# Adaptive-LayerNorm attention with a gated MLP on one core: banks of the MLP's products, the loads of its second half, and the order of attention's last unit

## The chip, the cores and the metric

The kernel runs on one core of one Trainium2 chip. The metric is the device time in microseconds, the median of several executions; before the change it is 2931.93 us over three runs (2928.81 to 2938.05).

## The reference

A transformer block in fp32 on 2048 tokens of width 576 (`x`). A vector `c` gives six modulation rows. Attention has 32 query heads and 16 key and value heads of width 128, and looks at the last 512 cached positions; the MLP has 4608 hidden columns.

```
mod = silu(c) @ w_mod                       # sa, ca, ga, sb, cb, gb
h = layernorm(x) * (1 + ca) + sa
q = h @ wq;  p = softmax(q k^T / sqrt(128)) # k, v: last 512 positions of the caches
x = x + ga * ((p v) @ wo)
h = layernorm(x) * (1 + cb) + sb
x = x + gb * ((relu(h @ W_gate) * (h @ W_up)) @ W_down)
```

## The kernel before

**Precision.** Each fp32 operand is split into a rounded part ("hi") and a remainder ("lo"), and a product is made of three matmuls: hi by hi, hi by lo, lo by hi. ScalarE (ACT) makes the hi parts, GpSimd (POOL) the lo parts.

**Order.** The order of the instructions of TensorE (PE), VectorE (DVE), ACT and POOL is written out by hand; DMA issues on the SP queue are placed by the framework, which also hands out tiles and sets the waits. A step with a time (`step(name, t, ...)`) runs when the main loop reaches that time; unit `u` has the times `10u` to `10u + 9`. `flush` runs the work that was put off in the lists `pend` (DVE) and `pend_act` (ACT).

**Attention** is 128 units, one for each head and block of 512 queries. The loop at the end of the kernel runs for unit `u`: the scores (`s_half`), their column maxima on DVE, the next unit's query projection (`qproj`), the spread of maxima and sums by a small matmul (`spread`, tile `qm`), the maxima as a row (`max_bc`, tiles r, rh, rr, mb, mr), the exponentials (`exp_half`; in the last unit the subtraction is itself a matmul with `mr`), the hi and lo parts of p, the column sums (`ksum_op`), and P times V of unit `u - 1` (`pv_half`, twelve matmuls: for each of four key tiles two with the hi and one with the lo part). `o_mul` scales the result, `o_hi` and `o_lo` split it.

The output projection of two heads is made in "pieces" of 128 queries (`piece`, `wo_piece`, `down_piece`: twelve matmuls of 288 columns into the one pair of banks of the pool psW). A piece is either added to the accumulator `acc` by DVE, or it is "seeded": ACT first copies `acc` into the banks (`put_seed`, line 617), the matmuls add to it, and ACT copies the result back (line 593). `seeded(n)` decides which.

**The last unit** (u = 127) has no next projection; the piece of unit 123 stands in its place, and then comes the spread. Both `pv_half` of unit 126 stand behind the spread. After the last unit come the first slots of the MLP, between which unit 127's own PV, sums, scaling and split are placed (steps `T.*`), and seven pieces that were left are "fillers", taken from a list by the MLP's first block.

**The MLP.** Two halves of 1024 tokens, each of 18 blocks of 256 hidden columns: `m` is 0 to 17 in the first half, 18 to 35 in the second (NFP = 18). Each block forms its 2 x 2 products by a scheme of seven, in the order P1, P6, P2, P7, P5, P4, P3, called slots 0 to 6. A slot is 14 matmuls of 512 columns (`prod`, line 928, tile `gu`), seven for the gate and seven for the up side, with pieces of the down projection of the block before between them (`md_piece`; in blocks 19 to 34 products of its own scheme, `st_tile`). `evac` and `evac_seeded` take the finished products out of PSUM. P2 goes on in P1's banks and P3 in P5's (`heir`). In blocks 1 to 17 P4 also goes on in P7's banks, and P6 and P7 begin from a copy that ACT makes of the product before them (`seed`, line 1104).

A product's pair of banks comes from psS (two pairs, called "s") or from psX (one pair, "x", which psM held during attention); psW's pair serves the pieces. `new_pair` decides which: before, x serves P4 in block 0; P6, P7 and P4 in the second half; and in blocks 1 to 17 P5 and P6, or P1 in P6's place after a block with a LayerNorm step, with P5 on s in such blocks (LN2 = 1, 2, 4, 6) and in block 17.

**Loads.** The weights of blocks 1 to 17 are read raw, split on chip (`w_split`, lines 705 to 707), and stored; block 0 and the second half read them split, one load of 640 KB for each product (`w_prep`, line 720, tile `wop`), two slots ahead. The seven operands of a half are five tiles each (`h_back`, line 832, tiles `hop`); those of the second half take the place of the first half's. `mat(m, i, fn)` puts a step behind slot `i` of block `m`, so that it runs in the middle of the next slot. Before, the seven `h_back(1, ...)` stand at slots 0 to 6 of block 17. In block 18 the finished rows of the first half are stored on SP too (line 647), each after its last add on DVE.

Of the kernel before, what the change touches and what calls it, by code (L numbers as in the profile page):

```python
# [7 lines left out]
F32 = mybir.dt.float32  # L8
# [6 lines left out]
P = 128  # L15
# [18 lines left out]
def kernel(  # L34
# [13 lines left out]
    nc = tc.nc  # L48
# [17 lines left out]
    psM = psM_scope.__enter__()  # L66
# [341 lines left out]
    NU = HKV * NQB * 2  # L408
# [6 lines left out]
    wqs, ks, vs, wos = {}, {}, {}, {}  # L415
# [3 lines left out]
    def unit(u):  # L419
        return UNITS[u]  # L420
# [21 lines left out]
    st_, t4, t5, pt, hi_, lo_, bc, rb, rinv, ks_, pvps, done, o, bps = ({} for _ in range(14))  # L442
# [98 lines left out]
    def ksum_op(u, h):  # L541
# [4 lines left out]
        else:  # L546
            for j in range(2):
                nc.gpsimd.tensor_tensor(ks_[u], ks_[u], p[:, j, :], op=ALU.add)  # L548

    def pv_half(u, h):  # L550
        g, qb, hd = unit(u)
        if h == 0:
            pvps[u] = psM.tile([P, 512], F32, tag="mm", name=f"pv{u}")
        ps, v, a, b = pvps[u], vs[g], hi_[u, h], lo_[u, h]
        for j in range(2):
            kt = 2 * h + j
            nc.tensor.matmul(ps, v[:, kt, :], a[:, j, :], start=(kt == 0), stop=False)
            nc.tensor.matmul(ps, v[:, 4 + kt, :], a[:, j, :], start=False, stop=False)
            nc.tensor.matmul(ps, v[:, kt, :], b[:, j, :], start=False, stop=(kt == 3))
        if h:  # L560
            done[u] = pvps.pop(u)
# [37 lines left out]
    def wo_piece(u1, qt, seed=None):  # L599
        g, qb, h = unit(u1)  # L600
        return down_piece([ohi[u1 - 1], ohi[u1]], [olo[u1 - 1], olo[u1]], [wos[h - 1], wos[h]],
                          4 * qb + qt, qt, f"wo{u1}_{qt}", seed=seed)
# [4 lines left out]
    w_use, pieces, seeds = set(), [], {}  # L607

    def seeded(n):
        return 0 < n < len(pieces) and (n - 1 in seeds or pieces[n - 1][0] % 10 == 6) and not any(pieces[n - 1][0] < t <= pieces[n][0] for t in w_use)  # L610

    def put_seed(n):
        if seeded(n):
            u1, qt = pieces[n][1:]
            g, qb, h = unit(u1)
            s = seeds[n] = psW.tile([P, 2, 512], F32, tag="w", name=f"wo{u1}_{qt}")
            nc.scalar.copy(s[:, :, :H2], acc[4 * qb + qt].rearrange("p (h n) -> p h n", h=2))

    def piece(n):
        add = wo_piece(*pieces[n][1:], seed=seeds.get(n))  # L620

        def end():
            add()
            put_seed(n + 1)

        (pend_act if n in seeds else pend).append(end)
        return n in seeds
# [7 lines left out]
    NFP = NFT // 2  # L635
# [5 lines left out]
    def md_piece(m, k, qt, pool=None):  # L641
# [4 lines left out]
        if fp == NFP - 1:  # L646
# [3 lines left out]
    OPS = {"P1": ("A11", "B11"), "P2": ("A12", "B21"), "P6": ("S2", "T2"), "P7": ("S3", "T3"),  # L650
           "P5": ("S1", "T1"), "P4": ("A22", "T4"), "P3": ("S4", "B22")}

    def order(m):
        return ("P1", "P6", "P2", "P7", "P5", "P4", "P3")
# [174 lines left out]
    def h_back(b, s):  # L829
        hs = hop[b, s] = [hp.tile([P, 512], F32R, tag="hT", name=f"hop{b}_{s}_{k}") for k in range(5)]  # L830
        for k in range(5):
            nc.sync.dma_start(hs[k][:96 if k == 2 else P].bitcast(F32), hkeep[b, s, k].bitcast(F32))
# [98 lines left out]
    LN2 = (1, 2, 4, 6)  # L931
# [154 lines left out]
    def new_banks(nm, k):  # L1086
        npair[0] += 1
        return (px["x"] if k == "x" else psS).tile([P, 2, 512], F32, tag=k, name=nm)

    def new_pair(m, s):  # L1090
        x = {"P4"} if not m else {"P6", "P7", "P4"} if m >= NFP else {"P1" if m - 1 in LN2 else "P6", "P5"}
        if m in LN2 or m == NFP - 1:
            x.discard("P5")
        pair[m, s] = new_banks(f"gu{npair[0]}", "x" if s in x else "s")

    def heir(m):
        return {"P2": "P1", "P3": "P5", **({"P4": "P7"} if 0 < m < NFP else {})}
# [227 lines left out]
    for i in range(1, len(VIS)):  # L1325
        g, qbs = VIS[i]
# [40 lines left out]
    for i, ab in enumerate(lay0 + lay):  # L1367
        n = i - len(lay0) - 2 * NFT + 4
# [4 lines left out]
    def mat(m, s, fn, sums=False):  # L1373
        mextra.setdefault((m, s, sums) if s < 6 else (m + 1, -1, sums), []).append(fn)
# [17 lines left out]
        mat(*at_, fn)  # L1392
    for i, fn in enumerate(sum(later.values(), [])):
        mat(7 + i // 5, (0, 1, 2, 4, 6)[i % 5], fn)
    for i, s in enumerate(order(1)):
        mat(NFP - 1, i, lambda s=s: h_back(1, OPS[s][1]))

    def sums(m, i):

# [12 lines left out]
    def mlp_slots():  # L1412
        for m in range(NB):
            two = m - 1 in ST
            if two:
                md = st_list(m - 1)
            else:
                md = [lambda k=k, qt=qt: md_piece(m - 1, k, qt) for k in range(2) for qt in range(4)] if m else []
            for i, s in enumerate(order(m)):
                early = 0 < m < NFP and not i  # L1420
                if not early:
                    flush_stores()
                if s in heir(m):
                    pair[m, s] = pair[m, heir(m)[s]]
                elif s not in seeds_of(m):
                    new_pair(m, s)
                prod(m, s, 7 * m + i, 0)
                if (m or i) and not early:
                    sums(m, i)
                    others(m, i)  # L1430
                if m in ST and i == 0:
                    sw_load(m)
                if two or m and i:
                    md.pop(0)()
                elif filler and not m:
                    filler.pop(0)()
                for fn in mextra.pop((m, i - 1, True), []):
                    fn()
                if two and i == 0:
                    if m - 1 in ST:  # L1440
                        sw_cut(m - 1, "T2")
                if two and i < 3:
                    st_sums(m - 1, (("S1", "S3"), ("S2",), ("S4",))[i])
                if m in ST:
                    sw_prep(m, i)
                prod(m, s, 7 * m + i, 1)
                wop.pop(7 * m + i)
                if early:
                    evac_seeded(m, s)
                    if put:  # L1450
                        put.pop()()
                    flush_stores()
                    sums(m, i)
                    others(m, i)
                if two or m and i < 2:
                    md.pop(0)()
                elif filler and not i:
                    filler.pop(0)()
                if not early:
                    (evac_seeded if 0 < m < NFP else evac)(m, s)  # L1460
                yield
        for k in range(2):
            for qt in range(4):
                if qt % 2 == 0:
                    st_end(k, qt // 2)
                md_piece(NB - 1, k, qt, (psS, "s") if qt % 2 else None)
        flush_stores()
        assert not mextra and not filler

    filler = [lambda q=q: wo_piece(NU - 3, q)() for q in (1, 2, 3)]  # L1470
    mlp = mlp_slots()

    def last_unit():
# [23 lines left out]
    t = 546  # L1497
    for s in ("P1", "P2", "P4", "P7", "P5", "P6", "P3"):
        for xx in range(2):
            for fn in w_later(s, xx, (xp, "xm", 640)):  # L1500
                step("w.l", t, fn)
                t = after(t + 8)
# [40 lines left out]
    def run(u, k):  # L1543
        t = 10 * u + k
        while sched and sched[-1][0] <= t:
            fn, args = sched.pop()[2:]
            fn(*args)
# [11 lines left out]
    for u in range(NU):  # L1559
        run(u, 0)  # L1560
        if u > 1 and u % 2 == 0:
            o_hi(u - 2)
            o_lo(u - 2)
        s_half(u, 0)
        s_half(u, 1)
        max_pre(u)
        if u:
            sum_pre(u - 1)
        run(u, 1)
        if u + 1 < NU:  # L1570
            qproj(u + 1, 0, 14)
        else:
            piece(at[10 * u + 1])
        run(u, 2)
        spread(u)
        max_bc(u)
        if u + 1 < NU:
            q_hi(u + 1)
        run(u, 3)
        if 10 * u + 3 in at:  # L1580
            piece(at[10 * u + 3])
        if u > 1 and u % 2:
            o_hi(u - 2)
            o_lo(u - 2)
        run(u, 4)
        if u:
            pv_half(u - 1, 0)
        if u + 1 == NU:
            pv_half(u - 1, 1)
        flush(pend_act)  # L1590
        exp_half(u, 0)
        flush()
        run(u, 5)
        exp_half(u, 1)
        if u:
            sum_bc(u - 1)
        if u + 1 < NU:
            q_lo(u + 1)
        ksum_op(u, 0)
        ksum_op(u, 1)  # L1600
        run(u, 6)
        if 0 < u < NU - 1:
            pv_half(u - 1, 1)
        if 10 * u + 6 in at:
            piece(at[10 * u + 6])
        run(u, 7)
        if u:
            o_mul(u - 1)
        flush()
        run(u, 8)  # L1610
        hi_half(u, 1)
        flush(pend_act)
        lo_half(u, 0)
        lo_half(u, 1)
        run(u, 9)
# [56 lines left out]
```

## Time and profile before

| | |
|---|---|
| median of three runs | 2931.93 us (2928.81 to 2938.05) |
| the profiled execution | 2930.85 us |
| its span, first to last instruction | 2929.1 us |
| TensorE busy | 2858.8 us, 98% of the span |
| VectorE, ScalarE, GpSimd busy | 73%, 51%, 72% |
| mean granted TensorE clock | 0.995 |
| DMA | 396.43 MB, 135 GB/s in the mean |

Idle time of TensorE counts first; a wait names the engine and line that ended it. A name such as `gu<-hop_T,wop` is the written tile and the read ones, with buffer numbers left out. L928 is line 928 of the kernel before. A matmul's recorded end is modelled and lies after the start of the next one.

### The profile page before, as it was taken

How to read it: one execution, taken by the hardware profiler on the slowest of the kernel's cores; microseconds unless marked ns; L12 is line 12 of the kernel's file. 1: busy time of each engine (PE TensorE's matmuls, PEld its weight loads, DVE VectorE, ACT ScalarE, POOL GpSimd, SP SyncE). 2: the span in 40 equal slices, each digit the busy share in tenths (PEclk: the TensorE clock that was granted, in tenths of full speed). 3: DMA queues.
4: the chain of work that ended last, by engine and by line, in shares of the span. 5: the costliest groups of instructions: out<-in, count | busy, mean ns of one | idle time of the engine just before them, and what ended most of it. 6: DMA issues, size and time to landing. Idle time of an engine off the chain costs nothing. (4 is left out here: it accounts for less than half of the span.)

```text
span 2929.1 us, 41284 instructions
## 1 busy us (share of the span) xinstructions
PE 2858.8 (98%) x15214; PEld 2488.3 (85%) x15214; DVE 2149.0 (73%) x2980; ACT 1489.0 (51%) x2097; POOL 2108.6 (72%) x1564
## 2 busy tenths in 40 slices
PE   6799999999999999999999999999999999999999
PEld 5688888888888888888888788888888888888888
DVE  7878888788878888777889655566676466666666
ACT  4466666666666666666756344443444122222221
POOL 5588888888888889876778666677777356656553
PEclk9899999999999999999999999999999999999999
DMA  4011222222223223322244456666667944444442
GB/s 150 22 45 55 83 93 84 67 99 93 92 83 106 90 63 133 101 70 85 65 146 133 135 209 219 225 231 223 234 227 245 327 160 152 151 152 152 158 151 104
DMA packets 162697, 396.43 MB, mean 135 GB/s; under 512 B 14912, under 2 KB 61760, under 8 KB 162496
## 3 DMA queue, kind: packets, MB, share of 16 engines
q1 hardware_dynamic: 131472, 282.15, 30.3%
q10 hardware_dynamic: 31024, 111.65, 9.7%
q8 instruction: 120, 1.97, 0.3%
q14 instruction: 81, 0.66, 0.1%
HBM read 268.73 MB, written 153.32 MB: 144 GB/s over the span
## 5 line engine op out<-in xcount | busy, mean ns | idle before, releaser
L539 POOL TENSOR_TENSOR lo<-p,hi 128x1024 fp32r<-128x1024 f32 x256 | 609.7, 2403 | 0.8 <-ACT hi L519 0.8
L548 POOL TENSOR_TENSOR ks<-ks,p 128x512 f32<-128x512 f32 x256 | 343.8, 1343 | 272.9 <-ACT p L532 207.6
L460 DVE TRANSPOSE_TENSOR_REDUCE t<-s 128x32 f32<-128x1024 f32 x256 | 316.4, 1243 | 135.2 <-PE s L457 123.9
L928 PE MATMUL gu<-hop_B,wop 128*128 128x512 f32 (+1 forms) x1512 | 378.4, 393 | 0.3 <-DMA wop<-wk_P 0.3
L928 PE MATMUL gu<-hop_T,wop 128*128 128x512 f32 (+1 forms) x1260 | 321.6, 395 | 2.2 <-DMA wop<-wk_P 2.2
L383 PE MATMUL qps<-hTa,wA 128*128 128x512 f32 x1288 | 312.5, 394 | 8.7 <-ACT lfa L365 7.4
L928 PEld LDWEIGHTS gu<-hop_B,wop 128*128 128x128 f32 (+1 forms) x1512 | 275.7, 188 | 52.7 <-ACT lflh L913 0.9
L584 PE MATMUL wo<-woga,ohi 128*128 128x288 f32 x1472 | 306.0, 301 | 1.5 <-DVE lfa L363 1.5
L383 PEld LDWEIGHTS qps<-hTa,wA 128*128 128x128 f32 x1288 | 244.7, 190 | 61.3 <-ACT lfa L365 7.8
L530 DVE TENSOR_TENSOR p<-s,mb 128x1024 f32<-128x1024 f32 x246 | 290.3, 1219 | 4.1
L519 ACT CAST hi<-p 128x1024 fp32r<-128x1024 f32 x256 | 268.9, 1050 | 7.1
L595 DVE TENSOR_TENSOR acc<-md,acc 128x576 f32<-128x576 f32 x160 | 120.9, 756 | 198.9 <-PE md L584 198.6
L928 PEld LDWEIGHTS gu<-hop_T,wop 128*128 128x128 f32 (+1 forms) x1260 | 228.9, 188 | 43.8 <-issue 2.4
L584 PE MATMUL md<-wogb,hhi 128*128 128x288 f32 x1280 | 261.5, 297 | 3.3 <-DVE acc L595 2.3
L532 ACT ACTIVATE p<-p 128x1024 f32<-128x1024 f32 x246 | 259.9, 1057 | 8.0 <-DVE p L530 7.9
L435 ACT ACTIVATE qhi<-qps 128x512 fp32r<-128x512 f32 x128 | 76.4, 597 | 340.6 <-PE qps L383 340.6
L584 PEld LDWEIGHTS wo<-woga,ohi 128*128 128x128 f32 x1472 | 238.7, 188 | 9.1 <-issue 1.9
L584 PEld LDWEIGHTS md<-wogb,hhi 128*128 128x128 f32 x1280 | 214.0, 189 | 16.0 <-DVE acc L595 3.1
L1039 DVE TENSOR_TENSOR acc<-st_P,acc 128x576 f32<-128x576 f32 x160 | 121.2, 757 | 134.7 <-PE st_P L1030 133.8
L584 PE MATMUL wo<-woga,olo 128*128 128x288 f32 x736 | 216.9, 295 | 0.3 <-POOL olo L573 0.2
L584 PE MATMUL md<-wogb,hlo 128*128 128x288 f32 x640 | 189.0, 295 | 0.0
L573 POOL TENSOR_TENSOR olo<-rb,ohi 128x512 fp32r<-128x512 f32 x128 | 166.6, 1301 | 23.7 <-ACT ohi L569 23.2
(263 smaller groups left out, 7084.9 us busy)
## 6 DMA issues: line engine op xcount, KB each, us to landing
wop<-wk_P SPq DMA_DIRECT2D x133, 640.0 KB
wk_P<-wop ACTq DMA_DIRECT2D x119, 640.0 KB
wr<-wlay SPq DMA_DIRECT2D x68, 384.0 KB
rogb<-wd SPq DMA_DIRECT2D x68, 288.0 KB
againq<-akq SPq DMA_DIRECT2D x18, 640.0 KB
rwA<-wq SPq DMA_DIRECT2D x32, 320.0 KB
wlay<-wg SPq DMA_DIRECT2D x36, 256.0 KB
roga<-wo SPq DMA_DIRECT2D x32, 288.0 KB
```

The lines of the kernel that those rows point to most:

```text
L383: return [lambda i=i, a=a, b=b: nc.tensor.matmul(ps, a, b, start=(i == 0), stop=(i == n - 1)) for i, (a, b) in enumerate(ops)]
L460: nc.vector.tensor_reduce(t4[u][:, 2 * h:2 * h + 2, :].rearrange("p k b -> p (k b)"), t.rearrange("p k (b j) -> p (k b) j", j=32), axis=AX ...
L519: nc.scalar.copy(hi_[u, h], pt[u, h])
L530: nc.vector.tensor_tensor(p, t, bc[u][:, None, :].to_broadcast([P, 2, 512]), op=ALU.subtract)
L532: nc.scalar.activation(p, p, AF.Exp, bias=0.0, scale=1.0)
L539: nc.gpsimd.tensor_sub(lo_[u, h], pt[u, h], hi_[u, h].bitcast(F32))
L548: nc.gpsimd.tensor_tensor(ks_[u], ks_[u], p[:, j, :], op=ALU.add)
L573: nc.gpsimd.tensor_sub(olo[u], o.pop(u), ohi[u].bitcast(F32))
L584: nc.tensor.matmul(ps[:, half, :H2], a[:, sl], w[b][:, cs], start=(n == 0 and seed is None), stop=(n == 5), skip_group_check=seed is not None)
L595: nc.vector.tensor_tensor(av, ps[:, :, :H2], av, op=ALU.add)
L928: nc.tensor.matmul(ps, a, c, start=s not in heir(m) and i == 0 and s not in seeds_of(m), stop=i == len(ops) - 1, skip_group_check=True)
L1039: nc.vector.tensor_tensor(t, ps[:, :, :H2], t, op=ALU.add)
```

## The change

Five edits. The second half's operands of P5, P4 and P3 are loaded later, behind slot 6 of block 17 and slots 0 and 1 of block 18; those of P1, P6, P2 and P7 stand behind slots 0, 1, 3 and 4 of block 17. `new_pair` gives x to P1 (and with it P2) in every block after block 0, and to P4 as well in block 0 and in the second half; all else is on s. In the last attention unit the eight hi matmuls of unit 126's PV are issued ahead of the spread and the four lo matmuls behind it; the last piece is no longer seeded; and block 0 takes no filler in slot 3 but two in slot 4.

```diff
+    def pv_part(u, lows):
+        g, qb, hd = unit(u)
+        if not lows:
+            pvps[u] = psM.tile([P, 512], F32, tag="mm", name=f"pv{u}")
+        ps, v = pvps[u], vs[g]
+        for kt in range(4):
+            a, b = (x[u, kt // 2][:, kt % 2, :] for x in (hi_, lo_))
+            if lows:
+                nc.tensor.matmul(ps, v[:, kt, :], b, start=False, stop=kt == 3)
+            else:
+                nc.tensor.matmul(ps, v[:, kt, :], a, start=kt == 0, stop=False)
+                nc.tensor.matmul(ps, v[:, 4 + kt, :], a, start=False, stop=False)
+        if lows:
+            done[u] = pvps.pop(u)
...
     def seeded(n):
-        return 0 < n < len(pieces) and (n - 1 in seeds or pieces[n - 1][0] % 10 == 6) and not any(pieces[n - 1][0] < t <= pieces[n][0] for t in w_use)
+        return 0 < n < len(pieces) - 1 and (n - 1 in seeds or pieces[n - 1][0] % 10 == 6) and not any(pieces[n - 1][0] < t <= pieces[n][0] for t in w_use)
...
     def new_pair(m, s):
-        x = {"P4"} if not m else {"P6", "P7", "P4"} if m >= NFP else {"P1" if m - 1 in LN2 else "P6", "P5"}
-        if m in LN2 or m == NFP - 1:
-            x.discard("P5")
+        x = ("P4",) if not m else ("P1", "P4") if m >= NFP else ("P1",)
...
-    for i, s in enumerate(order(1)):
-        mat(NFP - 1, i, lambda s=s: h_back(1, OPS[s][1]))
+    for (m, i), s in zip([(NFP - 1, i) for i in (0, 1, 3, 4, 6)] + [(NFP, 0), (NFP, 1)], order(1)):
+        mat(m, i, lambda s=s: h_back(1, OPS[s][1]))
...
-                elif filler and not m:
+                elif filler and not m and i != 3:
                     filler.pop(0)()
...
-                elif filler and not i:
+                elif filler and i in (0, 4):
                     filler.pop(0)()
...
             piece(at[10 * u + 1])
+            pv_part(u - 1, False)
         run(u, 2)
         spread(u)
...
         run(u, 4)
-        if u:
+        if u + 1 == NU:
+            pv_part(u - 1, True)
+        elif u:
             pv_half(u - 1, 0)
-        if u + 1 == NU:
-            pv_half(u - 1, 1)
```

## The prediction

> **What bounds the kernel now.** I read the page first, then the table of windows by stage (columns: stretch, length, busy time of PE, PEld, DVE, ACT and POOL with instructions, clock, DMA share, GB/s), then TensorE's waits inside the stages.
>
> ```profile
> PE 2858.8 (98%) x15214; PEld 2488.3 (85%) x15214; DVE 2149.0 (73%) x2980; ACT 1489.0 (51%) x2097; POOL 2108.6 (72%) x1564
> ...
> 200.00:1600.00 1400.00, 1395.94 (x7399) 1214.16 (x7399) 1153.55 (x1703) 940.88 (x1261) 1156.70 (x718) 1.00 0.28 90
> 1600.00:1675.00 75.00, 69.03 (x364) 58.40 (x363) 52.60 (x75) 32.56 (x46) 47.66 (x31) 1.00 0.41 130
> 1675.00:2270.00 595.00, 587.30 (x3231) 516.87 (x3230) 369.90 (x370) 257.69 (x360) 433.96 (x386) 1.00 0.64 227
> 2270.00:2345.00 75.00, 72.52 (x389) 63.62 (x388) 30.35 (x38) 13.35 (x19) 22.22 (x18) 0.98 0.89 321
> 2345.00:2900.00 555.00, 555.00 (x2965) 484.76 (x2965) 360.39 (x499) 136.73 (x258) 323.27 (x319) 1.00 0.47 151
> ```
>
> TensorE sets the end. Nothing can be won from 2345 on, where it never idles. The idle time that the edits can reach is the last attention unit with block 0 of the MLP (1600 to 1675: 5.97 us), blocks 1 to 17 (7.70 us) and the change of halves, blocks 17 and 18 (2.48 us). Who ended it, stage by stage (total us, times, longest; two waits of 0.5 us in the first stage follow below in their own rows):
>
> ```profile
> PE wo L584 <- ACT ohi L569: 1.6, 1, 1.6
> PE qm L483 <- DVE t L475: 1.3, 1, 1.3
> PE wo L584 <- ACT acc L593: 1.1, 1, 1.1
> PE wo L584 <- POOL olo L573: 0.8, 1, 0.8
> ...
> PE gu L928 <- ACT gu L1104: 5.2, 7, 1.4
> PE md L584 <- DVE acc L595: 2.3, 1, 2.3
> ...
> PE gu L928 <- DMA wop<-wk_P: 2.5, 2, 2.2
> ```
>
> **What one stall costs.** A recorded wait is too small, since a matmul's end lies after its successor's usual start. Block 9 hands over without a wait, block 14 with one:
>
> ```profile
> 1971.65 0.30 PE L584 MATMUL md<-wogb,hlo 128*128 128x288 f32 x1
> 1971.78 0.40 PE L928 MATMUL gu<-hy_T,wop 128*128 128x512 f32 x1
> ...
> 2151.16 0.29 PE L584 MATMUL md<-wogb,hlo 128*128 128x288 f32 x1
> 2152.13 0.50 PE L928 MATMUL gu<-hy_T,wop 128*128 128x512 f32 x1 [0.68 <-ACT gu L1104]
> ```
>
> Start to start is 0.13 and 0.97 us, a loss of 0.84 for a recorded 0.68, and the first matmul takes 0.50 instead of 0.40. So each stall costs its record plus 0.26 us.
>
> **Part 1, the last unit and block 0.** The last unit's chain, then the fillers:
>
> ```profile
> 1624.31 4.71 POOL L539 TENSOR_TENSOR lo<-p,hi 128x1024 fp32r<-128x1024 f32 x2
> 1626.72 0.45 PE L483 MATMUL qm<-t,quad 128*128 128x80 f32 x2 [1.34 <-DVE t L475]
> 1627.21 0.22 DVE L498 TENSOR_REDUCE r<-qm 128x16 f32<-128x64 f32 x1 [0.54 <-PE qm L483]
> 1627.51 1.54 DVE L505 CAST rh<-r 128x16 fp32r<-128x16 f32 x1
> 1630.79 1.19 PE L526 MATMUL s<-mr,minus 128*128 128x512 f32 x4 [0.50 <-ACT mr L511]
> 1631.16 0.63 ACT L593 COPY acc<-wo 128x576 f32<-128x576 f32 x1
> 1631.83 0.64 ACT L617 COPY wo<-acc 128x576 f32<-128x576 f32 x1
> 1632.52 0.54 PE L584 MATMUL wo<-againo,ohi 128*128 128x288 f32 x2 [0.54 <-ACT wo L617]
> ...
> 1637.10 0.40 PE L584 MATMUL wo<-againo,ohi 128*128 128x288 f32 x1 [1.11 <-ACT acc L593]
> ...
> 2368.27 1.62 PE gu L928 x7
> ...
> L595 DVE TENSOR_TENSOR acc<-md,acc 128x576 f32<-128x576 f32 x160 | 120.9, 756 | 198.9 <-PE md L584 198.6
> ```
>
> Moving the eight high matmuls of unit 126's PV ahead of the spread: seven such matmuls issue in 1.62 us, so eight take 1.85 us from 1625.4 (1626.72 less the wait of 1.34), and the spread (qm) starts at 1627.2, not 1626.7. The wait of 1.34 is filled, but the chain to the subtraction (qm, r, rh, mr, s) begins 0.5 us later, and only four PV matmuls are left to cover it. What saves it is rh: 1.54 us for 16 columns, ending at 1629.05, just behind the POOL pair that ends at 1629.02. I read it as held by POOL; then a later r is free and s still starts at 1630.79. Value 0, bounds 0 and 0.5 us lost.
>
> The Trainium skill (SBUF — State Buffer, "SBUF: two separate sides") calls the pair of ports that VectorE and GpSimd share an exclusive lock, taken for a whole instruction by whichever comes first. By that rule the sum has 0 here, without it 0.5 us lost; the trace agrees with it in the two ends, 1629.05 and 1629.02.
>
> The last piece unseeded: ACT's copy (L617, 0.64 us) goes, and the piece can start when L593 ends, at 1631.8 to 1631.9 instead of 1632.52: 0.6 us. Its sum goes from ACT, where the copy out stood behind both exponentials, to a DVE add (L595) behind o_mul. So the first filler of block 0 no longer waits: 1.11 + 0.26 = 1.4 us.
>
> Slot 3's filler waits for unit 127's ohi and olo (1.63 + 0.81 recorded, 2.44). It moves behind two halves of a product, 2 x 1.62 = 3.24 us of other matmuls, which covers 2.44: 2.44 + 2 x 0.26 = 3.0 us. What is late next: two fillers in slot 4 are now one half (1.62 us) apart on psW's single pair, and the second waits for the first's DVE add, 0.76 us with its start some 0.3 us behind the matmul; it fits by 0.5 us. Block 0's P5 evacuation on DVE then stands behind that second add; P3, which accumulates on P5's bank, needs it a slot later. Part 1: 0.6 + 1.4 + 3.0 = 5.0 us; bounds 3 and 5.
>
> **Part 2, banks in blocks 1 to 17.** P6's start is a seed: ACT copies P1's bank into P6's. Two seeds, block 14 (P6 on the x pair) and block 5 (P6 already on psS, because block 4 ran the LayerNorm):
>
> ```profile
> 2148.30 0.84 ACT L705 CAST wop<-ws 128x768 fp32r<-128x768 f32 x1 [4.06 <-DVE ws L735]
> 2151.08 1.00 ACT L1104 COPY gu<-gu 128x1024 f32<-128x1024 f32 x1 [1.94 <-DVE u L1077]
> ...
> 1824.59 1.00 ACT L1104 COPY gu<-gu 128x1024 f32<-128x1024 f32 x1 [0.70 <-PE gu L928]
> 1825.77 0.62 ACT L1067 CAST hhi<-u 128x512 fp32r<-128x512 f32 x1 [0.19 <-DVE u L1077]
> ```
>
> In block 14 the seed waits for DVE's u, the evacuation of the previous block's P3, which held the x pair. In block 5 it starts off PE while u is still to come (1825.77): P6 took the bank that P4 left a slot earlier. The change gives every block that order: P1 on x (free since P2, slot 2), P6, P7, P5 in turn on psS. P7 then inherits P3's bank, a whole slot later. So all seven recorded waits should go: 5.2 + 7 x 0.26 = 7.0 us. Two things can hold some back. ACT runs L705, which waits for DVE's ws, ahead of the seed, and in block 14 it ended at 2149.14; unheld, P6 would start at 2151.29, so a seed of 1.00 us must start by 2150.3, a slack of 1.1 us; and DVE, gaining nothing, stays as late as it is. Bounds 2 and 7; I take 6.3, nearer to the block 5 row. The 2.3 us wait of md for DVE's acc is not touched: 0, bounds 2.6 either way, since it hangs on how VectorE and POOL happen to meet.
>
> **Part 3, the change of halves.** The stall is P6's operand wop, late behind operand loads on SP:
>
> ```profile
> 2286.71 2.37 SPq L832 DMA_DIRECT2D hop_T<-hk_T  x2
> 2290.98 0.32 SPq L720 DMA_DIRECT2D wop<-wk_P  x1
> 2292.20 3.99 SPq L832 DMA_DIRECT2D hop_T<-hk_T  x5
> ...
> 2290.00:2298.00 8.00, 5.80 (x30) 4.56 (x28) 2.84 (x4) 1.64 (x2) 1.29 (x1) 1.00 1.04 385
> 2298.00:2302.00 4.00, 3.71 (x12) 3.15 (x13) 0.00 (x0) 0.00 (x0) 0.00 (x0) 0.60 1.03 362
> ```
>
> One operand is four loads of 256 KB and one of 192 KB (the code's shapes), 1.25 MB, or 3.2 us at the 385 GB/s of that row. The new order takes T1 out from ahead of this wop, so it lands about 3.2 us sooner; it was 2.2 us late. Both waits go: 2.5 + 2 x 0.26 = 3.0 us. After the stall TensorE ran at a mean clock of 0.60 for 4 us: another (1 - 0.60) x 4 = 1.6 us. Together 4.6 us.
>
> The Trainium skill (TensorE: Matmul & The Clock Gate, "What's actually happening") has the clock halve after an idle window of about 3.4 us. By it a 2.2 us wait would have cost itself alone and this part be 3.0 us; the trace disagrees (0.60 behind a 2.2 us wait), and I keep 4.6.
>
> What is late next: in block 18 three operands, 3 x 1.25 MB, stand among four wop loads (0.66 MB each), the out stores, which wait on SP for DVE's adds, and a wogb load. At 385 GB/s the operands add about 3.2 us of queue to each slot of some 4.8 us. A wop is issued about two slots ahead, so I expect it to fit narrowly. Value 4.2; bounds 1 and 4.6.
>
> **The second half's banks.** P1 moves to x, which P4 leaves. P4's last reader in one block, and the next block's P1:
>
> ```profile
> 2567.60 0.69 DVE L1077 SCALAR_TENSOR_TENSOR srb<-srb,gu 128x512 f32<-128x512 f32 x1
> 2570.07 0.63 PE L928 MATMUL gu<-hop_B,wop 128*128 128x512 f32 x2
> ```
>
> The reader ends at 2568.29, 1.8 us ahead of P1: no cost. P6, P7 and P5 on psS have longer.
>
> **Sum.** 5.0 + 6.3 + 4.2 = 15.5 us from the profiled execution's 2930.85 us (span 2929.1 and 1.75 around it): 2915.4. That execution lies 1.1 us under the median, 2931.93, so I write 2916.
>
> **Rivals.**
> 1. VectorE and POOL set the pace of blocks 1 to 17, and part 2 yields its lower bound 2 while the rest comes: 2930.85 - 5.0 - 2 - 4.2, about 2920. For it: ws in 4.06 us of ACT idling above. Against: block 9 has no wait, and POOL is busy 434 of 595 us.
> 2. The operand loads of block 18 make a later wop late (P5 or P4), with a fresh clock drop: part 3 falls to 0, 2930.85 - 11.3, about 2920. With rival 1 too, 2924: no difference that could be told. About 0.3% (8.8 us) is what this measurement tells from none.
> 3. The change does not do what it says: the allocator hands P6 the bank of P3, not P4's. Part 2 is 0: about 2922. The block 5 rows speak against it.
> 4. Slower: in the second half P4's evacuation lands after the next P1. It decides from 1.8 us of delay. If DVE's evacuation slips by 3.3 us, two adds of 0.75 us beyond that, all 17 blocks pay 1.5 + 0.26: 30 us, twice what is won, 2915.4 + 30, about 2945. Against: TensorE has no wait there in 555 us, and DVE is busy only 360.
>
> **Numbers.** Forecast 0.62; rival 1 alone 0.12, rival 2 alone 0.09, both 0.06, rival 3 0.04, rival 4 or another new wait 0.07. Faster by over 0.3% (below 2923.1): 0.62 + 0.12 + 0.09 less a little of each edge, 0.80; within 0.3%: 0.13; slower: 0.07. The forecast's best case, 5.0 + 7.0 + 4.6 + 2.6 = 19.2, gives 2911.6, and the runs of before reach 3 us under their median: low 2909. High 2928, with rivals 1 and 2 both and one md wait more.
>
> **What would show it.** L483's wait gone and s still near 5.4 us behind the piece before it; no waits for L617, L593, ohi or olo in block 0; L1104 released by PE in every block; no wop wait and a clock of 1.00 at the change of halves; 0 idle in the second half. It is wrong if L1104 still waits for u, if wop waits return in block 18, or if gu waits for DVE in the second half.

## The result and the profile after

The changed kernel takes 2920.61 us in the median (2916.08 to 2925.96), the kernel before 2932.45 beside it: ratio 0.9958, 95% interval 0.9942 to 0.9974. It is faster, by 11.8 us where the forecast had 16, and inside the range. A later measurement of the same kernel gave 2920.13 (2916.42 to 2921.20), ratio 0.9963 (0.9949 to 0.9977).

The execution profiled first took 2925.96 us, with a span of 2923.5. In the changed kernel every line behind the new function stands 15 further down, those behind the rewritten choice of banks 13 (the product L928 is L943, md and wo L584 are L599, the DVE add L595 is L610, the DVE sums L735 are L750, POOL's wop L706 and L707 are L721 and L722, the seed L1104 is L1117, DVE's u L1077 is L1092). Below, a "seed wait" is a wait of TensorE for that copy by ACT, an "md wait" one for the banks of a down-projection piece (tile md), and a "wop wait" one for a product's weights (tile wop). The table of windows by stage, columns as before:

```profile
1600.00:1675.00 75.00, 72.89 (x381) 62.79 (x380) 55.90 (x79) 34.41 (x48) 52.02 (x32) 0.98 0.47 151
1675.00:2270.00 595.00, 590.00 (x3235) 519.90 (x3234) 384.50 (x369) 259.80 (x362) 440.54 (x387) 0.99 0.63 226
2270.00:2345.00 75.00, 74.10 (x409) 65.30 (x408) 31.25 (x41) 13.22 (x20) 23.30 (x20) 1.00 0.90 327
2345.00:2900.00 555.00, 555.00 (x2969) 485.04 (x2968) 361.14 (x501) 136.16 (x256) 323.15 (x320) 1.00 0.46 150
```

TensorE's idle time falls from 5.97 to 2.11 us in the first stage, from 7.70 to 5.00 in the second, and from 2.48 to 0.90 in the third, which makes 8.1 us; in the fourth it is still 0. But the clock, 1.00 in the first two stages before, is now 0.98 and 0.99. TensorE's waits in the first three stages:

```profile
PE pv L558 <- POOL lo L539: 1.1, 1, 1.1
PE s L526 <- ACT mr L511: 1.0, 1, 1.0
...
PE md L599 <- DVE acc L610: 4.7, 2, 2.3
PE gu L943 <- DMA wop<-wk_P: 0.9, 1, 0.9
PE gu L943 <- POOL wop L722: 0.2, 1, 0.2
```

The seven waits for ACT's seed (5.2 us before) are gone, and so are block 0's three and the one of 2.2 us for wop. The md wait for DVE's add, one of 2.3 us before, now stands there twice. In the last unit, waits of 1.1 and 1.0 us stand where 1.3 and 0.5 stood. The seed of block 14, which waited for DVE's u in the prediction's rows, now starts off TensorE while u is still to come:

```profile
2150.00 1.00 ACT L1117 COPY gu<-gu 128x1024 f32<-128x1024 f32 x1 [0.59 <-PE gu L943]
2151.30 0.62 ACT L1082 CAST hhi<-u 128x512 fp32r<-128x512 f32 x1 [0.30 <-DVE u L1092]
```

So it is in every block: P6's seed waited for u in 8 of 17 blocks before, and is released by TensorE in all 17 now.

Where the gain lies is read from starts, since busy times hide the clock. Five points of TensorE's timeline in the kernel before: the first score matmul of unit 127, the first product of block 0, the end of block 0's last product, slot 6 of block 17, and the end of block 18's last product.

```profile
1620.88 0.39 PE L455 MATMUL s<-qhi,againk 128*128 128x512 f32 x1
...
1634.22 0.85 PE L928 MATMUL gu<-hop_B,wop 128*128 128x512 f32 x3
...
1675.02 1.10 PE L928 MATMUL gu<-hop_B,wop 96*128 96x512 f32 x4
...
2285.79 0.86 PE L928 MATMUL gu<-hop_B,wop 128*128 128x512 f32 x3
...
2330.17 1.09 PE L928 MATMUL gu<-hop_B,wop 96*128 96x512 f32 x4
```

The same points in a second profiled execution of the changed kernel (2919.17 us, span 2917.4; the run e8 below):

```profile
1621.44 0.39 PE L455 MATMUL s<-qhi,againk 128*128 128x512 f32 x1
...
1634.30 0.85 PE L943 MATMUL gu<-hop_B,wop 128*128 128x512 f32 x3
...
1670.71 1.10 PE L943 MATMUL gu<-hop_B,wop 96*128 96x512 f32 x4
...
2279.07 0.86 PE L943 MATMUL gu<-hop_B,wop 128*128 128x512 f32 x3
...
2318.93 1.10 PE L943 MATMUL gu<-hop_B,wop 96*128 96x512 f32 x4
```

Their differences, with those of the first profile (the same five points there are 1623.90, 1637.74, 1674.14, 2284.01 and 2325.06):

| stretch, us | before | after, first profile | after, second profile | second less before | forecast |
|---|---|---|---|---|---|
| up to unit 127 | 1620.88 | 1623.90 | 1621.44 | +0.56 | 0 |
| last unit | 13.34 | 13.84 | 12.86 | -0.48 | -0.6 |
| block 0 | 40.80 | 36.40 | 36.41 | -4.39 | -4.4 |
| blocks 1 to 17 | 610.77 | 609.87 | 608.36 | -2.41 | -6.3 |
| change of halves | 44.38 | 41.05 | 39.86 | -4.52 | -4.2 |
| rest | 598.93 | 598.44 | 598.47 | -0.46 | 0 |
| span | 2929.1 | 2923.5 | 2917.4 | -11.7 | -15.5 |

One stretch falls well short, blocks 1 to 17. Three other things differ between two executions of one program: the start-up, which the change doesn't touch (3.0 us later in the first, 0.6 in the second), the last unit, and the change of halves.

**Why blocks 1 to 17 fall short.** Block 8 in the second profile, VectorE's timeline:

```profile
1949.26 1.23 DVE L1139 TENSOR_TENSOR c<-gu,u 128x1024 f32<-128x1024 f32 x1 [0.92 <-PE gu L943]
1950.52 0.69 DVE L1140 SCALAR_TENSOR_TENSOR c<-c 128x512 f32<-128x512 f32 x1
1951.12 6.06 DVE L750 TENSOR_TENSOR wr<-wr,wr 128x768 f32<-128x768 f32 x1
1957.11 0.74 DVE L610 TENSOR_TENSOR acc<-md,acc 128x576 f32<-128x576 f32 x1
```

POOL's in the same time:

```profile
1950.55 1.26 POOL L721 TENSOR_TENSOR wop<-wr,wop 32x256 fp32r<-32x256 f32 x1 [1.82 <-ACT wop L720]
1951.77 1.28 POOL L722 TENSOR_TENSOR wop<-wr,wop 128x512 fp32r<-128x512 f32 x1
1953.02 1.42 POOL L182 TENSOR_TENSOR wogb<-rogb,wogb 128x576 fp32r<-128x576 f32 x1
1954.41 1.28 POOL L1083 TENSOR_TENSOR hlo<-c,hhi 128x512 fp32r<-128x512 f32 x1
1955.65 0.71 POOL L721 TENSOR_TENSOR wop<-wr,wop 32x256 fp32r<-32x256 f32 x1
1956.34 1.97 POOL L722 TENSOR_TENSOR wop<-wr,wop 128x512 fp32r<-128x512 f32 x1
```

And TensorE's:

```profile
1957.91 0.54 PE L599 MATMUL md<-wogb,hhi 128*128 128x288 f32 x2 [2.33 <-DVE acc L610]
```

The sum of the weights' third quarter (wr on wr, 128x768) takes 0.94 to 0.95 us in 15 of its 17 places in this profile and 6.05 or 6.06 in two, in blocks 8 and 10; in the kernel before it is 6.06 in block 10 alone. Here it starts 0.57 us into a row of POOL instructions without a gap. Going by its own 0.95 us, an estimate, it gets through only at the last change between them, at about 1956.23; the POOL sum that starts there takes 1.97 us where the same form takes 1.28. The add of the last md piece stands behind it on VectorE, the one pair of md banks stays taken, and the next md piece waits 2.33 us. Slot 6 of block 8 is 2.61 us longer than before: the record plus 0.28. In block 10 the same wait was there before, and the slot is still 1.53 us longer. That is the clock:

```profile
1957.16:1960.57 3.41, 2.66 (x17) 2.49 (x18) 2.91 (x5) 1.46 (x2) 2.54 (x3) 1.00 0.59 238
...
2032.26:2035.67 3.41, 3.41 (x12) 2.87 (x11) 0.97 (x2) 0.84 (x2) 3.19 (x3) 0.50 0.90 312
```

Behind block 8's wait (first row) it is 1.00, behind block 10's 0.50 for 3.41 us. So 2.61 + 1.53 = 4.1 us were given back, and what is left for the removed seeds is 2.4 + 4.1 = 6.5, a remainder. In the first profile, with a half clock behind both waits, 4.00 + 1.52 = 5.5 us were given back.

### The profile page after: what moved, and what is told of

It is laid out like the page before. It is cut to its first block, busy times and chain, and to the rows that moved or that the text cites. A ratio compares the mean times of both kernels' runs of the same rounds, so it can differ in the third digit from the quotient of the medians.

```text
span 2923.5 us, 41266 instructions
## 1 busy us (share of the span) xinstructions
PE 2858.1 (98%) x15214; PEld 2490.0 (85%) x15214; DVE 2161.4 (74%) x2981; ACT 1489.4 (51%) x2095; POOL 2117.4 (72%) x1564
## 3 DMA queue, kind: packets, MB, share of 16 engines
q8 instruction: 120, 1.97, 0.3%
## 5 line engine op out<-in xcount | busy, mean ns | idle before, releaser
L943 PE MATMUL gu<-hop_B,wop 128*128 128x512 f32 (+1 forms) x1512 | 379.0, 394 | 0.9 <-DMA wop<-wk_P 0.9
L943 PEld LDWEIGHTS gu<-hop_B,wop 128*128 128x128 f32 (+1 forms) x1512 | 276.3, 188 | 53.6 <-issue 1.3
L943 PE MATMUL gu<-hop_T,wop 128*128 128x512 f32 (+1 forms) x1260 | 319.9, 393 | 0.0
L599 PE MATMUL wo<-woga,ohi 128*128 128x288 f32 x1472 | 305.9, 301 | 1.5 <-DVE lfa L363 1.5
L599 PE MATMUL md<-wogb,hhi 128*128 128x288 f32 x1280 | 263.4, 298 | 5.8 <-DVE acc L610 4.9
L943 PEld LDWEIGHTS gu<-hop_T,wop 128*128 128x128 f32 (+1 forms) x1260 | 228.4, 188 | 41.0
L610 DVE TENSOR_TENSOR acc<-md,acc 128x576 f32<-128x576 f32 x160 | 120.9, 756 | 177.5 <-PE md L599 177.1
L599 PEld LDWEIGHTS wo<-woga,ohi 128*128 128x128 f32 x1472 | 238.7, 188 | 9.1 <-issue 1.9
L599 PEld LDWEIGHTS md<-wogb,hhi 128*128 128x128 f32 x1280 | 214.9, 190 | 19.1 <-DVE acc L610 6.3
L599 PE MATMUL wo<-woga,olo 128*128 128x288 f32 x736 | 216.9, 295 | 0.3 <-POOL olo L588 0.2
L599 PE MATMUL md<-wogb,hlo 128*128 128x288 f32 x640 | 190.1, 297 | 0.0
```

The lines of the kernel that those rows point to most:

```text
L599: nc.tensor.matmul(ps[:, half, :H2], a[:, sl], w[b][:, cs], start=(n == 0 and seed is None), stop=(n == 5), skip_group_check=seed is not None)
L943: nc.tensor.matmul(ps, a, c, start=s not in heir(m) and i == 0 and s not in seeds_of(m), stop=i == len(ops) - 1, skip_group_check=True)
```

## The experiments

**Each part alone.** The banks, on the kernel before:

```diff
-        x = {"P4"} if not m else {"P6", "P7", "P4"} if m >= NFP else {"P1" if m - 1 in LN2 else "P6", "P5"}
-        if m in LN2 or m == NFP - 1:
-            x.discard("P5")
+        x = ("P4",) if not m else ("P1", "P4") if m >= NFP else ("P1",)
```

> The kernel before with the banks alone (P1 and P2 on x). Theory: the banks take away the seven seed waits (7.2 us by the slots' lengths), and nothing of the banks themselves makes TensorE wait elsewhere; the md waits of 2.3 us in slot 6 come from DVE's sum S3 being held by POOL for 6.06 us, in whatever block the two happen to meet. Then no seed wait is left, and the time falls by 7.2 us less 1.5 to 4 us for each block in which a 6.06 us sum is found (none to two): 2925 to 2931. Rival: the banks give TensorE its gain back by themselves, since the blocks' period is set by VectorE and POOL: then the freed time comes back as waits for POOL's or ACT's wop in most blocks, not in slot 6 of one or two, and the time stays within 2 us of before.

Measured 2925.84 us, ratio 0.9981 (0.9972 to 0.9991). Its waits from 1675 to 2345:

```profile
PE md L584 <- DVE acc L595: 2.6, 2, 2.3
PE gu L928 <- DMA wop<-wk_P: 2.6, 1, 2.6
```

No seed wait is left, and blocks 1 to 17 are 6.2 us shorter than in the kernel before, against part 2's 6.3. The md wait of 2.3 us is in block 10, as before; block 8 has one of 0.32.

The operand loads, on the kernel before:

```diff
-    for i, s in enumerate(order(1)):
-        mat(NFP - 1, i, lambda s=s: h_back(1, OPS[s][1]))
+    for (m, i), s in zip([(NFP - 1, i) for i in (0, 1, 3, 4, 6)] + [(NFP, 0), (NFP, 1)], order(1)):
+        mat(m, i, lambda s=s: h_back(1, OPS[s][1]))
```

> The kernel before with the later operand loads alone. Theory: P6's weight load no longer waits behind two operands, so its 2.2 us wait and the half clock behind it go; the wait of P1's load, 0.28 us before, stays, since that load still stands behind the third and fourth operand. Blocks 17 and 18 get 3.5 to 4 us shorter, and the time falls by as much (about 2928.5). Rival: the loads moved into block 18 make a later weight load wait there, and the time falls by under 1 us.

Measured 2930.35, ratio 0.9987 (0.9979 to 0.9996). The waits in the same stretch:

```profile
PE gu L928 <- ACT gu L1104: 6.2, 7, 1.5
PE md L584 <- DVE acc L595: 2.3, 1, 2.3
```

The wop waits are gone, P1's of 0.28 too, which was expected to stay. From the start of block 17 to the end of 18 it takes 3.7 us less, and 4.5 less in the table's stretch from slot 6 of block 17. The md wait is still one of 2.3, but in block 8, not 10, and with a half clock behind it: this edit touches neither the banks nor anything before block 17's loads, and the wait has moved all the same. So it is not the banks alone that place it.

The last unit, on the kernel before (the PV in two parts, the last piece unseeded; block 0's fillers as they were):

```diff
+            pv_part(u - 1, False)
...
-        if u:
+        if u + 1 == NU:
+            pv_part(u - 1, True)
+        elif u:
             pv_half(u - 1, 0)
-        if u + 1 == NU:
-            pv_half(u - 1, 1)
...
-        return 0 < n < len(pieces) and (n - 1 in seeds or pieces[n - 1][0] % 10 == 6) and not any(pieces[n - 1][0] < t <= pieces[n][0] for t in w_use)
+        return 0 < n < len(pieces) - 1 and (n - 1 in seeds or pieces[n - 1][0] % 10 == 6) and not any(pieces[n - 1][0] < t <= pieces[n][0] for t in w_use)
```

> The kernel before with the last attention unit's edits alone (PV in two parts, last piece unseeded). Theory: the two parts gather the unit's idle time into one stretch of 2 us right behind the spread, the clock halves there for 3.4 us, and block 0 starts 0.5 us later against the start of the unit than before; slot 0 is then 1.4 us shorter because the last piece is unseeded. Net 0.9 us. Rival: the half clock in the changed kernel's profile was a chance of that one execution: block 0 starts 0.6 us earlier, net 2.0 us.

Measured 2931.68, ratio 0.9995 (0.9985 to 1.0005). The last unit takes 12.84 us and slot 0 of block 0 is 1.36 shorter, together 1.9; the run as a whole can't be told from no change. The waits of 1.1 and 1.0 us (pv for POOL's lo, s for ACT's mr) are there as in the first profile of the changed kernel, but no half clock behind them. So the new place of the PV does not by itself make the half clock; the last section shows what goes with it. This profile has no md wait at all, and no sum of 6.06 us in any block, on the old banks. The edit of block 0's fillers was not run alone; its worth is read from the slots of block 0.

The changed kernel with the PV back in its old place, run twice:

```diff
-            pv_part(u - 1, False)
...
-        if u + 1 == NU:
-            pv_part(u - 1, True)
-        elif u:
+        if u:
             pv_half(u - 1, 0)
+        if u + 1 == NU:
+            pv_half(u - 1, 1)
```

> The changed kernel with the last unit's PV back behind the spread in one piece (unseeded last piece, fillers, banks and loads kept). Theory: the waits are 1.3 and 0.5 us apart again, no half clock in the last unit, and block 0 starts 1.1 to 1.3 us earlier against the unit's start than in the changed kernel. Rival: the unseeded piece makes the half clock, not the PV in two parts: it stays, and block 0 starts no earlier.

> The changed kernel with the PV of the last unit in its old place, once more. Its first profile had the 2.34 us md wait in block 10 alone (0.38 in block 8), while both profiles of the changed kernel have it in 8 and 10. If the place of that wait belongs to the program, block 8's sum takes 0.95 us here again and the median is 2917 to 2919, some 2 us under the changed kernel; if it belongs to the execution, block 8 may show 6.06 us, and the medians are the same.

Measured 2918.28, ratio 0.9948 (0.9935 to 0.9962), and 2917.25, ratio 0.9949 (0.9935 to 0.9962). The last unit takes 12.82 and 12.81 us, against 12.86 in the second profile of the changed kernel: the place of the PV is worth nothing there. Both profiles have the held sum in block 10 alone. Block 8 in the second of them, VectorE and then POOL:

```profile
1951.08 0.95 DVE L750 TENSOR_TENSOR wr<-wr,wr 128x768 f32<-128x768 f32 x1
```

```profile
1951.57 1.05 POOL L721 TENSOR_TENSOR wop<-wr,wop 32x256 fp32r<-32x256 f32 x1 [1.82 <-ACT wop L720]
1952.59 1.29 POOL L722 TENSOR_TENSOR wop<-wr,wop 128x512 fp32r<-128x512 f32 x1
```

The sum starts within 0.04 us of where it starts in the changed kernel, but POOL's row begins at 1951.57 instead of 1950.55, after the start of the sum and not before it. That one microsecond decides between 0.95 and 6.06.

The changed kernel again:

> The changed kernel itself once more, profiled again: what of its profile is the kernel's and what the execution's. The seed waits should be absent again. If the half clock behind the 2.34 us md wait and in the last unit depends on the execution, one of the three windows (last unit, block 8, block 10) is missing or has moved here; if it depends on the kernel, all three return at the same places. The same for the 3.0 us by which the last unit started later than in the kernel before. Median 2918 to 2922.

Measured 2920.13, ratio 0.9963 (0.9949 to 0.9977). The held sums return in blocks 8 and 10, as they return in block 10 alone in the pair of runs above: in two programs the place was the same twice. But the kernel with the later loads, which is the kernel before up to block 17, has its held sum in block 8 and not in 10, and of the kernel before there is one profile; what places the sum stays open. The half clock is there behind block 10 only, and not in the last unit; the start-up is 0.56 us later than before and not 3.0; P1's wop wait of 0.9 is absent. These belong to the execution.

**Moving the held sum.** The sum is issued one slot earlier, behind the md piece, on the changed kernel and on the one before:

```diff
-        for k, s in {1: [(0, "S1")], 2: [(0, "S4")], 5: [(1, "S3")], 6: [(1, "S2")]}.get(i, []):
+        for k, s in {1: [(0, "S1")], 2: [(0, "S4")], 6: [(1, "S2")]}.get(i, []):
...
+                if i == 4 and m + 1 < NFP:
+                    w_sums(m + 1, "S3")
```

> The changed kernel with one edit: the sum of the third quarter of the weights (DVE, line 750, 128x768 on wr), which runs beside the evacuation of P4's product and held DVE for 6.06 us in one block of the changed kernel's profile (0.95 us is its median), is issued one slot earlier, behind the slot's md piece. Theory A: the 2.34 us waits of md for DVE's add in blocks 8 and 10 come from this sum, which POOL holds off; then no sum on wr lasts 6 us, both waits go (5.5 us by the slots: 4.00 and 1.52), any clock drop behind them goes too, and blocks 1 to 17 come to about 604 us against 609.6: median about 2915. Rival B: POOL holds whichever two-input operation of DVE stands there; then another sum (ws) or the c of line 1140 lasts several us instead, a seed or a wop is late, and the median stays at 2919 to 2922. Rival C: the sum ahead of the evacuation of P5 makes that late, and P3, which accumulates on its bank, waits: 0.5 us a block or more, 2925 or above.

> The kernel before with the same single edit of the sum. By theory A only block 10's md wait (2.34 + 0.26 us) goes: about 2.6 us under the kernel before, ratio 0.9991, with the seven seed waits still there. By rival B no difference or a new wait of like size; by rival C slower by 5 us or more. If both this and the edit of the changed kernel gain, the md wait is a cost of its own that the change of banks neither makes nor removes.

Measured 2920.73, ratio 0.9967 (0.9954 to 0.9980), and 2940.30, ratio 1.0033 (1.0020 to 1.0047). On the changed kernel the 2.3 us waits go, but the time does not. The waits from 1675 to 2300:

```profile
PE gu L943 <- POOL wop L722: 1.0, 5, 0.4
PE md L599 <- DVE acc L610: 1.0, 3, 0.6
```

The groups of VectorE there (busy, mean ns of one):

```profile
L750 DVE TENSOR_TENSOR ws<-wr,wr 128x768 f32<-128x768 f32 x16 | 55.8, 3486 | 0.0
L1140 DVE SCALAR_TENSOR_TENSOR c<-c 128x512 f32<-128x512 f32 x17 | 38.8, 2281 | 0.6
L750 DVE TENSOR_TENSOR wr<-wr,wr 128x768 f32<-128x768 f32 x16 | 28.3, 1772 | 0.0
```

The means were 3023 (ws), 1788 (c) and 1585 ns (wr) in the second profile of the changed kernel. The c and the ws now take longer, and the moved sum itself is not free: it takes 1.7 to 4.0 us in ten of its 17 places instead of 6.06 in two. From block 1's first product to slot 6 of 17 it is 606.7 us, against 608.1; this profiled execution loses 1.2 us in the last unit, by a half clock there. Rival B is the right one: other operations are held, and small waits stand in several blocks. On the kernel before, the same edit takes the md wait of 2.3 us away too and costs 8.8 us. Its waits from 1675 to 2345:

```profile
PE gu L928 <- ACT gu L1104: 14.1, 10, 3.3
PE gu L928 <- DMA wop<-wk_P: 1.6, 1, 1.6
PE md L584 <- DVE acc L595: 0.5, 2, 0.3
```

The seed waits grow from 5.2 us in seven to 14.1 in ten, and the moved sum is held in 13 of 17 places (1.3 to 4.3 us). What ends the wait in block 6, ACT's timeline and then TensorE's (1.43 us in the kernel before):

```profile
1867.67 1.00 ACT L1104 COPY gu<-gu 128x1024 f32<-128x1024 f32 x1 [3.96 <-DVE u L1077]
```

```profile
1868.72 0.50 PE L928 MATMUL gu<-hy_T,wop 128*128 128x512 f32 x1 [3.31 <-ACT gu L1104]
```

With the old banks a later VectorE (u, L1077) is a later seed, and TensorE waits. With the new ones no seed waits for u, here or in any of the nine profiles with these banks. The same edit costs 8.8 us on the one (2940.30 less 2931.46) and 0.6 on the other (2920.73 less 2920.13), all measured side by side; those figures include the md waits of 2.3 us that the edit takes away, one on the kernel before and two on the changed one.

The sum on POOL, on the changed kernel, on it with the old place of the PV, and on the kernel before:

```diff
-        nc.vector.tensor_tensor(flat(out), flat(a), flat(b), op=op)
+        (nc.gpsimd if s == "S3" else nc.vector).tensor_tensor(flat(out), flat(a), flat(b), op=op)
```

> The changed kernel with one edit: the third-quarter sum (line 750, 128x768 on wr) runs on POOL instead of DVE, in the same place of the program. In the runs so far it takes DVE 0.95 us, or 6.06 us where it starts inside a back-to-back run of POOL; on POOL, whose 128x512 sums take 1.28 us, I estimate 1.9 us. Theory A: the md waits of blocks 8 and 10 come from VectorE standing still behind POOL in this one sum; with it off VectorE, both go (2.61 and 1.53 us of slot time in the second profile of the changed kernel), nothing else of VectorE is held as long there, and POOL, 434 busy of 595 us, has room for 17 x 1.9 us: median 2914 to 2917. Rival B: the wait only moves, since POOL's own wop (line 722) is now 1.9 us later behind the sum, or another sum of VectorE is held: wop waits on POOL of 0.3 us or more in most blocks, median 2919 to 2925.

> The same with the PV of the last unit in its old place behind the spread. By theory A and a value of 0 to 0.5 us for that place: 2913 to 2917, the fastest of all; by rival B as the run before it, 2919 to 2925.

> The kernel before with the sum on POOL. By theory A block 10's md wait goes (2.6 us), and the seed waits, which hang on VectorE's u, stay or shrink: 2925 to 2929. By rival B the seed waits grow, as they did with the sum one slot earlier (14.1 us against 5.2): 2932 to 2942. What the change of banks is worth is then the distance to the changed kernel with the same edit: about 8 to 12 us if the seeds stay, more if they grow.

Measured 2930.55, ratio 0.9995 (0.9986 to 1.0004); 2931.05, ratio 0.9995 (0.9986 to 1.0004); and 2949.20, ratio 1.0060 (1.0047 to 1.0073). All of the gain is lost. The waits of the first from 1675 to 2300:

```profile
PE md L599 <- DVE acc L610: 6.2, 9, 0.9
PE gu L943 <- POOL wop L722: 4.5, 12, 1.5
```

and of the last:

```profile
PE gu L928 <- ACT gu L1104: 17.3, 12, 3.3
PE md L584 <- DVE acc L595: 3.2, 7, 0.9
```

The sum takes 1.84 us on POOL, near the estimate of 1.9, and POOL is busy 468 of 600 us in the first of them, so it isn't full; but TensorE now waits for POOL's wop twelve times instead of once, and VectorE's ws, which waits for the sum (9.9 us of VectorE's idle time ahead of ws end with POOL's wr), comes later still. Half of theory A holds: the md waits of 2.3 us come from this sum. Each of the nine sums of 6.06 us in the seven profiles that have one stands with such a wait in its block, and where no sum is that long no such wait is left. What is refuted twice over is that this sum alone is the cost: when it is moved, waits come back at other places. With VectorE and POOL meeting in another order, the distance between the kernel before and the changed one, 11 to 12 us, is 19.6 with the sum one slot earlier (2940.30 less 2920.73) and 18.7 with it on POOL (2949.20 less 2930.55).

**All that seemed to gain.** The changed kernel with the old place of the PV, the sum one slot earlier, and one operand load moved from block 17 to 18:

```diff
-    for (m, i), s in zip([(NFP - 1, i) for i in (0, 1, 3, 4, 6)] + [(NFP, 0), (NFP, 1)], order(1)):
+    for (m, i), s in zip([(NFP - 1, i) for i in (0, 1, 3, 6)] + [(NFP, 0), (NFP, 1), (NFP, 2)], order(1)):
```

> The changed kernel with three edits: the third-quarter sum one slot earlier; the PV of the last unit in its old place; operand loads of the second half at slots 0, 1, 3 and 6 of block 17 and 0, 1 and 2 of block 18 instead of 0, 1, 3, 4 and 6 of 17 and 0 and 1 of 18. The third edit takes one operand load out from ahead of P1's wop, 1.25 MB or about 3.2 us at the 385 GB/s of the change of halves, against a wait of 0.90: the wait goes (1.2 us). If theory A and this hold, median 2911 to 2914, below both kernels. If the load that moved to block 18 makes P5's or P4's wop late there, a wait of 1 to 2 us stands in block 18 instead and the median is 2914 to 2917.

Measured 2918.86, ratio 0.9963 (0.9950 to 0.9976): no better than the PV's old place alone, and above the 2911 to 2917 that was expected. P1's wop is 1.31 us late here although one load fewer stands ahead of it, so the wait of 0.90 us did not come from that load; its cause stays open. Of the kernels run, the changed one with the PV in its old place has the lowest medians, some 2 to 3 us under the changed kernel's; their intervals overlap, so the order of the two isn't settled.

## Why the prediction was right, step by step

**Part 1** held. Block 0 gained 1.38 us in slot 0 (1.4 was written) and 4.58 less 1.60 = 2.98 by moving slot 3's filler (3.0): slot 3 is 4.58 us shorter and slot 4, with two fillers, 1.60 longer. Those two do fit one after the other, with no wait. The unseeded piece gave 0.5 (0.6). For the PV ahead of the spread 0 was right, and for the reason given: s starts 9.91 us behind the start of the unit, as before, and rh, which starts 0.24 us later, takes 1.30 us instead of 1.54 and still ends with POOL's pair (1632.07 and 1632.04 in the first profile). The rule drawn on there, from the Trainium skill (SBUF — State Buffer, "SBUF: two separate sides"), gave 0 as well, and the trace agrees. What the step missed is that the two waits left, 1.13 and 0.99 us, now end 1.7 us apart, and in two of the five profiles with this edit the clock halved behind them: 1.0 us in the first profile of the changed kernel (13.84 against 12.86), and 1.2 with the sum one slot earlier.

**Part 2** had the right mechanism and, for the seeds, the right size: 6.5 us against 6.3, and 6.2 with the banks alone. P6's seed waits for u in none of the 17 blocks, where it did in 8, so rival 3, that the allocator picks P3's bank, is excluded. The term that was wrong is the one written at 0 with bounds of 2.6 us: "The 2.3 us wait of md for DVE's acc is not touched". It cost 4.1 us, past its bound: a second such wait in block 8, 2.61, and a half clock of 1.53 behind the one in block 10. The reason given for the bounds, how VectorE and POOL happen to meet, was the right one; what was left out is that a wait can come twice, and that a clock drop can follow it, though the prediction itself had priced one at the change of halves. 2916 + 4.1 is 2920.1, against the 2920.6 measured; that it comes so near is partly luck, since the later start (+0.56) and the shorter rest (-0.46), which the prediction doesn't have, happen to cancel.

**Part 3**, 4.2 us, measured 4.5 in the second profile; 3.3 in the first, with a wop wait of 0.90 us. The late load feared in block 18, P5's or P4's (rival 2), did not come in either; the one that did is that of P1 of block 18, issued in block 17, and only in some executions.

**The second half** stayed without idle time up to its last block, where one wait of 0.9 us stands before and after, so rival 4 is out. Rival 1 named almost the measured time, 2920, but not by its own way: it had the seeds held back by ACT and VectorE, and they are all gone. That its time fits is luck; where it was right is the pair of engines. A slower VectorE no longer reaches TensorE by the seeds, but by md's single pair of banks, and a later POOL by its wop.

## What to carry to other kernels

A chain that hands a bank from one engine to the next can make TensorE pay for delays of an engine that is far from full; choosing the bank that was left longest ago took 6.2 to 6.5 us out, and an edit that cost the old plan 8.8 then cost 0.6. The new plan isn't proof against every such edit: the sum on POOL cost it about 10 us. Where two engines hold each other off, moving one operation to another place or to the other engine can move the wait with it, as it did twice here: look for the stage's whole sequence before betting on the one long row. And profile a program twice before a 1 to 3 us stall is called its own.

## What the runs showed of the hardware

**A sum of VectorE with both inputs in SBUF may be held through a whole row of POOL instructions.** The 6.06 us in block 8 span four complete POOL instructions and parts of two more, while VectorE's adds with one input in PSUM (acc, L610) keep a mean of 754 to 756 ns and a longest of 759 in every profile. In the eleven profiles in which VectorE makes this sum, 143 of the 187 sums start with POOL idle and take at most 0.95 us; 42 start inside a POOL instruction and take 1.26 to 6.06; the other two start in the last 0.15 us of one and take 0.95 and 0.97. The Trainium skill (SBUF — State Buffer, "SBUF: two separate sides") says that the engine that comes first has the shared pair for the whole instruction. The traces agree that the first one decides, by those counts and by the pair above (1951.08 against 1951.57, and 1951.12 against 1950.55), but the loser waited for five POOL instructions, the rest of the first and four whole ones. Why it got through at the last change and at none of the four before isn't shown.

**The clock is judged in fixed windows.** The two half clocks of blocks 8 and 10 in the first profile of the changed kernel start 75.10 us apart (1960.98 and 2036.08), which is 22 windows of 3.414; each lasts 3.41. In all 14 profiles every change of the granted clock lies on such a grid of 3.41 us, to within 0.01, and where the grid starts differs from one execution to the next. Cut on that grid, the window before the second one and the one after it (columns as above):

```profile
2032.65:2036.06 3.41, 1.07 (x5) 0.61 (x4) 3.41 (x3) 0.09 (x1) 3.41 (x3) 1.00 0.91 366
2036.08:2039.49 3.41, 3.41 (x14) 3.28 (x14) 1.72 (x3) 1.45 (x2) 2.53 (x4) 0.50 0.56 206
```

In the kernel before, on its own grid (counted back from its half clock at 2298.77), the same wait of block 10 falls across two windows:

```profile
2032.52:2035.93 3.41, 2.46 (x11) 1.69 (x9) 3.41 (x1) 1.33 (x2) 3.41 (x4) 1.00 0.93 313
2035.93:2039.34 3.41, 2.02 (x14) 1.97 (x15) 2.92 (x5) 1.20 (x2) 2.53 (x2) 1.00 0.60 239
2039.34:2042.75 3.41, 3.41 (x17) 2.77 (x16) 2.47 (x4) 0.27 (x1) 2.49 (x3) 1.00 0.80 275
```

The whole wait of 2.34 us in one window leaves TensorE 1.07 us busy, and the next window runs at half; split in two, 2.46 and 2.02 us remain and the clock stays. From unit 127 on, in the 14 profiles, the twelve windows with 2.04 us or more of recorded waiting were all followed by a half clock, of nine between 1.61 and 1.87 four were, and none below that started one. This is why the same wait costs 2.6 us in one execution and 4.0 in the next (slot 6 of block 8: 7.43 and 8.82 us): the phase of the grid differs. The Trainium skill (TensorE: Matmul & The Clock Gate, "What's actually happening") puts the drop behind an idle window of about 3.4 us; the length agrees with the 3.41 here, but here windows with 2.04 us or more of recorded waiting were always enough, and one of 1.61 was too.
